# Attention into two feed-forward layers: one planner that also hands out six PSUM banks, new ranks, and another order of the first steps

## The chip, the cores and the metric

The kernel runs on one core of a Trainium2 chip. The metric is the device time of one execution in microseconds; the median of three runs of the kernel before is 1122.49 us (1120.99 to 1125.56). The core has five engines with a queue each: TensorE (PE, matrix products, with its weight loads shown as PEld), VectorE (DVE), ScalarE (ACT), GpSimd (POOL) and SyncE (SP, which here issues all DMAs). Matrix products land in PSUM, eight banks of 512 fp32 columns; the other data is in SBUF.

## The reference

Attention over batch 4, 8 heads, 576 positions, head size 64, with a decay that is added to the scores, and then two feed-forward layers over the 2304 tokens (512 to 2048 to 512, and 512 to 1536 to 512 with a gate). Cut to what matters:

```python
cum = np.cumsum(np.log(np.clip(f, 0.0001, 1.0)), axis=-1)
scores = scale * q @ k.T
scores = np.where(causal, -1e9, scores + cum[:, :, :, None] - cum[:, :, None, :])
scores = scores - scores.max(-1)
attn = np.exp(scores); attn = attn / (attn.sum(-1) + 1e-9)
x = attn @ v                              # then tokens x 512
h = x @ w_in;  x = (h * sigmoid(1.702 * h)) @ w_out
x = (silu(x @ w_gate) * (x @ w_val)) @ w_out2
```

The weights come in 64-bit floats, which the kernel turns into two fp32r parts (a high one and the rest) by itself.

## The kernel before

**Attention, by pairs of heads.** A pair P (0 to 15) holds two heads of one batch, in the two halves of the partitions; e is the head in the pair. `maxima(P)` records the work that finds the row maxima. Keys and queries come by DMA (`raw`), ACT casts them to a high part (`hi`, L264) and POOL subtracts for the rest (`lo`, L265). TensorE multiplies queries and keys and adds the decays `dk` (L272, L275) in four chunks of columns; all four use the one tile `mx` of two banks (one for each head). For each chunk DVE takes masked maxima out of the banks (L279, L295) into the tile `mt`. Then TensorE transposes `mt` with an identity ("turn", L308), once more into `mx`, and ACT copies the result to `selm` (L311). Since there is one `mx`, each chunk waits until DVE has read the one before, the turn waits for the last maxima, and the next pair's first chunk waits for ACT's copy.

`products(P)` records what uses the maxima: scores in four chunks with the decays and maxima as a fourth product (L326), into four banks `sc` used in turn; `exp` on ACT (L331); causal masks on POOL (L335); products with the values into `xx` (L356), row sums by a product with ones into the free columns of `xx` (L385); copies out of `xx` (L368, L389); and the division: sums to `rs` by DMA, a reciprocal on DVE (L400, L401), to DRAM and back spread over partitions (`rw`, `rb`), a product and a split into `xhi` and `xlo` (L408 to L411).

**The order.** Both functions only record operations with an engine, a duration, a rank, what they read and write, and a latency (`Program.add`). `Program.order` is a list scheduler: it keeps a clock for each engine and gives it, among the operations that are ready, the one with the lowest rank. The rank is P for products and P - 1.25 for maxima. The order that comes out is each engine's instruction order. The first steps (the logarithm of `f`, its running sum, its two parts `ahl`, and the DMAs that spread them to `dk`, as well as the table `selc` made by four transposes, L207 and L210) are recorded the same way.

**Weights.** Five weight tiles (of the 13 that fit) are loaded and converted during attention with a rank behind all else (`early`): a DMA of 512 KB, an absolute value on ACT (L461), four DVE operations (L463 to L468), a cast on ACT (L481) and a subtraction on POOL (L482). They may start at 100 us plus 12 us each by the scheduler's clock.

**The two feed-forward layers** (`moe`, L512 to L564) start when the sums of pair 15 are through TensorE. All tokens pass four chunks of four column tiles, later four of three, three fp32r products each; their weights are loaded and converted on the way. Nothing of this part is edited but the step size of a weight's conversion in `load_w`.

Of the kernel before, what the change touches and what calls it, by code (L numbers as in the profile page):

```python
# [17 lines left out]
NH = B * H  # L18
# [8 lines left out]
LOOK = 1.25  # L27
QH = 378
WHEN, WSTEP = 100000, 12000
# [9 lines left out]
class Program:  # L39
# [3 lines left out]
    def __init__(self):  # L43
        self.ops = []
        self.writer = {}
        self.readers = {}

    def add(self, eng, dur, rank, emit, reads=(), writes=(), lat=None, after=0):
        n = len(self.ops)
        deps = set()  # L50
        for k in reads:
            if k in self.writer:
                deps.add(self.writer[k])
# [12 lines left out]
        self.ops.append((eng, dur, rank, emit, sorted(deps), lat, after))  # L66

    def order(self):
# [40 lines left out]
def kernel(  # L109
# [18 lines left out]
    def f32(ap):  # L128
        return ap.bitcast(F32)
# [14 lines left out]
    prog = Program()  # L144
# [6 lines left out]
    NK, NR, NP, NV, NX, NB = 2, 2, 3, 2, 3, 2  # L151
# [6 lines left out]
    m5 = tiles(2, [128, 2], F32, "m5")  # L158
# [6 lines left out]
    rs = tiles(2, [128, 9], F32, "rs")  # L165
    rr = tiles(2, [128, 9], F32, "rr")
# [3 lines left out]
    da = pd.tile([NH, 2, S], F32, name="da")  # L170
# [7 lines left out]
    half = (slice(0, 64), slice(64, 128))  # L178

# [3 lines left out]
    def sp(rank, o, i, reads, writes, lat):  # L183
        add("sp", DMA_ISSUE, rank, lambda: nc.sync.dma_start(out=o, in_=i), reads, writes, lat=lat)
# [5 lines left out]
    sp(-9, ft, f, (), ["ft", ("xs", 0)], 2200)  # L190
    add("pool", 200, -9, lambda: nc.gpsimd.memset(zero, 0.0), (), ["zero", ("p", 2, 0)])
    add("pool", 300, -9, lambda: nc.gpsimd.affine_select(
        out=mk, in_=zero, pattern=[[-1, 128]], compare_op=ALU.is_ge, fill=NEG, base=0, channel_multiplier=1),
        ["zero"], ["mk", ("p", 2, 0)])
    add("pool", 500, -9, lambda: nc.gpsimd.affine_select(
        out=ident, in_=zero, pattern=[[-1, 128]], compare_op=ALU.not_equal, fill=1.0, base=0, channel_multiplier=1),
        ["zero"], ["ident", ("p", 2, 0)])
    add("dve", 1400, -9, lambda: nc.vector.memset(f32(mt), 0.0), (), ["mt0"])
    for q in range(4):
        for c in (4 * q, 66 + 4 * q):  # L200
            add("dve", 80, -9, lambda q=q, c=c: nc.vector.memset(f32(mt[:, q, :, c:c + 2]), 1.0), ["mt0"], [("mt1", q, c)])
    MT1 = [("mt1", q, c) for q in range(4) for c in (4 * q, 66 + 4 * q)]
    add("dve", 220, -9, lambda: nc.vector.tensor_copy(out=identr, in_=ident), ["ident", ("p", 2, 0)], ["identr"])

    def selectors():
        for q in range(4):
            nc.tensor.matmul(mx[:, q * 128:(q + 1) * 128], mt[:, q, 0, :], identr, start=True, stop=True)  # L207

    add("pe", 600, -9, selectors, ["identr"] + MT1, [("mx", 0)])
    add("act", 600, -9, lambda: nc.scalar.copy(out=selc.rearrange("p a b -> p (a b)"), in_=mx[:, 0:512]), [("mx", 0)], ["selc"])  # L210
    add("dve", 450, -9, lambda: nc.vector.memset(xx[:, 0:384], 0.0), (), ["xs0"])
    add("dve", 220, -9, lambda: nc.vector.memset(maskw[:, 0:384], 0.0), (), ["maskw0"])
    add("dve", 220, -9, lambda: nc.vector.tensor_copy(out=maskw[:, 384:512], in_=mk), ["mk", ("p", 2, 0)], ["maskw"])
    add("dve", 540, -10, lambda: nc.vector.memset(one, 1.0), (), ["one", ("xs", 1)])
    add("dve", 540, -10, lambda: nc.vector.tensor_scalar(
        out=ft, in0=ft, scalar1=1e-4, scalar2=1.0, op0=ALU.max, op1=ALU.min), (), ["ft", ("xs", 0)])
    add("act", 2000, -10, lambda: nc.scalar.activation(out=lf, in_=ft, func=AF.Ln), ["ft"], ["lf", ("xs", 2)])
    add("dve", 1350, -10, lambda: nc.vector.tensor_tensor_scan(
        out=cum, data0=one, data1=lf, initial=0.0, op0=ALU.mult, op1=ALU.add),
        ["one", "lf", ("xs", 1), ("xs", 2)], ["cum", ("rb", 0, 0)])  # L220
    add("dve", 520, -10, lambda: nc.vector.tensor_scalar(
        out=ft, in0=cum, scalar1=-8.0, scalar2=None, op0=ALU.mult), ["cum", ("rb", 0, 0)], ["ft", ("xs", 0)])
    add("dve", 800, -10, lambda: nc.vector.tensor_copy(out=ahl[0], in_=ft), ["ft", ("xs", 0)], ["ahl0", ("selm", 0)])
    add("dve", 750, -10, lambda: nc.vector.tensor_tensor(
# [442 lines left out]
```

## Time and profile before

| | |
|---|---|
| median of three runs | 1122.49 us |
| the profiled execution, its own time | 1123.12 us |
| its span, first to last instruction | 1121.1 us |
| attention (0 to the first product of the layers) | 265.8 us |
| the two layers | 855.3 us |
| TensorE busy | 1048.3 us, 94% |
| DVE, ACT, POOL busy | 623.2, 360.8, 182.4 us |

The profiled execution has 2.0 us outside its span and lies 0.6 us above the median. The layers keep TensorE at work nearly without a gap, the attention stage does not. For matrix products the view's durations overlap their neighbours, as they are pipelined; the distance between two starts is what one costs.

### The profile page before, as it was taken

How to read it: one execution, taken by the hardware profiler on the slowest of the kernel's cores; microseconds unless marked ns; L12 is line 12 of the kernel's file. 1: busy time of each engine (PE TensorE's matmuls, PEld its weight loads, DVE VectorE, ACT ScalarE, POOL GpSimd, SP SyncE). 2: the span in 40 equal slices, each digit the busy share in tenths (PEclk: the TensorE clock that was granted, in tenths of full speed). 3: DMA queues.
4: the chain of work that ended last, by engine and by line, in shares of the span. 5: the costliest groups of instructions: out<-in, count | busy, mean ns of one | idle time of the engine just before them, and what ended most of it. 6: DMA issues, size and time to landing. Idle time of an engine off the chain costs nothing.

```text
span 1121.1 us, 15630 instructions
## 1 busy us (share of the span) xinstructions
PE 1048.3 (94%) x6212; PEld 860.2 (77%) x6212; DVE 623.2 (56%) x1227; ACT 360.8 (32%) x648; POOL 182.4 (16%) x262
## 2 busy tenths in 40 slices
PE   2888777889999999999999999999999999999998
PEld 1666656667688788878877888888888888888886
DVE  5456756552966835664485578337733863363333
ACT  1455444443524313332343343123212321221110
POOL 4333343331201100200020011002100210010000
PEclk9999888999999999999999999999999999999999
DMA  3133353210221300220021012002200220000101
GB/s 121 45 103 114 97 165 105 96 47 23 79 72 38 113 1 1 75 75 1 19 95 37 1 57 95 1 1 77 93 1 1 88 82 1 1 0 29 48 19 75
DMA packets 25464, 61.43 MB, mean 55 GB/s; under 512 B 7760, under 2 KB 8272, under 8 KB 25392
## 3 DMA queue, kind: packets, MB, share of 16 engines
q1 hardware_dynamic: 25392, 60.45, 17.0%
q8 instruction: 48, 0.79, 0.3%
q14 instruction: 24, 0.20, 0.1%
HBM read 55.35 MB, written 4.94 MB: 54 GB/s over the span
## 4 chain that ended last, share of the span: by engine, by line
PE 80%; DVE 12%; ACT 2%; issue 2%; DMA 2%; POOL 1%; SPq 1%; ACTq 0%; DVEq 0%; POOLq 0%
PE ps L513 22%; PE ps L514 22%; PE ps L512 22%; PE sc L326 5%; PE xx L356 4%; PE mx L272 2%; DVE cvt L466 2%; DVE junk L279 2%; PE xx L385 2%; DVE cvt L468 2%; PE mx L275 1%; DVE cvt L464 1%; DVE cvt L463 1%; DVE g L526 1%; DVE s L534 1%
## 5 line engine op out<-in xcount | busy, mean ns | idle before, releaser
L512 PE MATMUL ps<-xhi,w 128*128 128x512 f32 (+1 forms) x800 | 294.5, 368 | 0.0
L513 PE MATMUL ps<-xlo,w 128*128 128x512 f32 (+1 forms) x800 | 294.4, 368 | 0.0
L514 PE MATMUL ps<-xhi,w 128*128 128x512 f32 (+1 forms) x800 | 294.2, 368 | 0.0
L513 PE MATMUL ps<-g,w 128*128 128x512 f32 (+1 forms) x560 | 207.5, 371 | 3.1 <-DVE g L526 3.1
L512 PE MATMUL ps<-g,w 128*128 128x512 f32 (+1 forms) x560 | 206.1, 370 | 3.7 <-ACT g L525 3.6
L514 PE MATMUL ps<-g,w 128*128 128x512 f32 (+1 forms) x560 | 206.1, 368 | 0.5 <-POOL w L482 0.5
L482 POOL TENSOR_TENSOR w<-cvt,w 128x512 fp32r<-128x512 f32 x68 | 89.4, 1319 | 664.8 <-ACT w L481 648.4
L532 ACT ACTIVATE t<-ps 128x512 f32<-128x512 f32 (+1 forms) x140 | 77.5, 554 | 298.4 <-PE ps L514 297.5
L512 PEld LDWEIGHTS ps<-xhi,w 128*128 128x128 f32 x800 | 150.8, 189 | 25.2
L514 PEld LDWEIGHTS ps<-xhi,w 128*128 128x128 f32 x800 | 150.8, 188 | 25.1
L513 PEld LDWEIGHTS ps<-xlo,w 128*128 128x128 f32 x800 | 150.8, 189 | 24.9
L534 DVE SCALAR_TENSOR_TENSOR s<-t,ps 128x512 f32<-128x512 f32 (+1 forms) x140 | 88.4, 631 | 123.9 <-ACT t L532 123.0
L525 ACT CAST g<-s 128x512 fp32r<-128x512 f32 (+1 forms) x140 | 81.0, 578 | 182.9 <-DVE s L546 129.4
L513 PEld LDWEIGHTS ps<-g,w 128*128 128x128 f32 x560 | 105.6, 189 | 24.5 <-DVE g L526 7.4
L512 PEld LDWEIGHTS ps<-g,w 128*128 128x128 f32 x560 | 105.4, 189 | 24.6 <-ACT g L525 7.3
L559 DVE SCALAR_TENSOR_TENSOR acc<-ps,acc 128x512 f32<-128x512 f32 (+1 forms) x120 | 76.0, 636 | 84.9 <-PE ps L514 84.2
L526 DVE TENSOR_TENSOR g<-s,g 128x512 fp32r<-128x512 f32 (+1 forms) x140 | 92.0, 658 | 54.1 <-ACT g L525 53.4
L514 PEld LDWEIGHTS ps<-g,w 128*128 128x128 f32 x560 | 105.6, 189 | 17.9 <-POOL w L482 0.9
L279 DVE CUSTOM_DVE_ANT_0 junk<-mx,maskw 128x512 bf16<-128x512 f32 (+3 forms) x128 | 61.8, 483 | 38.2 <-PE mx L275 36.2
L331 ACT ACTIVATE p<-sc 128x512 f32<-128x512 f32 (+2 forms) x128 | 56.4, 504 | 34.9 <-PE sc L326 34.6
L335 POOL TENSOR_SCALAR_AFFINE_SELECT p<-p 128x128 f32<-128x128 f32 (+1 forms) x160 | 43.9, 290 | 144.7 <-ACT p L331 143.6
L546 DVE TENSOR_TENSOR s<-s,ps 128x512 f32<-128x512 f32 (+1 forms) x60 | 38.0, 633 | 46.0 <-PE ps L514 45.7
(70 smaller groups left out, 1029.5 us busy)
## 6 DMA issues: line engine op xcount, KB each, us to landing
raw<-in_kq_dram SPq DMA_DIRECT2D x16, 576.0 KB
stg<-in_w_dram SPq DMA_DIRECT2D x16, 512.0 KB
stg<-in_w1o_dram SPq DMA_DIRECT2D x16, 512.0 KB
stg<-in_wg_dram SPq DMA_DIRECT2D x12, 512.0 KB
stg<-in_wv_dram SPq DMA_DIRECT2D x12, 512.0 KB
stg<-in_w2o_dram SPq DMA_DIRECT2D x12, 512.0 KB
vr<-in_v_dram SPq DMA_DIRECT2D x16, 320.0 KB
rb<-rw SPq DMA_DIRECT2D x32, 144.0 KB
```

What stands on the lines that cost most here:

```text
L279: nc.vector.tensor_tensor_reduce(out=junk[:, 0:n], in0=mx[:, e * 512 + o:e * 512 + o + n], in1=maskw[:, end - n:end], scale=1.0, scalar=fl ...
L326: nc.tensor.matmul(bank[e][:, o:o + n], w[half[e]], x[half[e]], start=w.tensor is h_.tensor and x.tensor is h_.tensor, stop=x.tensor is sm ...
L331: nc.scalar.activation(out=ps[e][:, a:z], in_=sc[c % 2][e][:, 0:z - a], func=AF.Exp, scale=0.125)
L482: nc.gpsimd.tensor_tensor(out=w[:, 1, :], in0=st, in1=f32(w[:, 0, :]), op=ALU.subtract)
L512: nc.tensor.matmul(o, wh, rh, start=i == 0, stop=False)
L513: nc.tensor.matmul(o, wh, rl, start=False, stop=False)
L514: nc.tensor.matmul(o, wl, rh, start=False, stop=i == n - 1)
L525: nc.scalar.copy(out=g[:, 0, 0:n], in_=s)
L526: nc.vector.tensor_tensor(out=g[:, 1, 0:n], in0=s, in1=f32(g[:, 0, 0:n]), op=ALU.subtract)
L532: nc.scalar.activation(out=t, in_=o, func=AF.Tanh, scale=scale)
L534: nc.vector.scalar_tensor_tensor(out=s, in0=t, scalar=1.0, in1=o, op0=ALU.add, op1=ALU.mult)
L559: nc.vector.scalar_tensor_tensor(out=a, in0=o, scalar=0.5, in1=a, op0=ALU.mult, op1=ALU.add)
```

## The change

The change has four parts. (1) The tiles `mx` and `sc` go; six banks are given out by the scheduler itself: an operation can take banks and give them back, at most four for maxima or for scores (`CAP`), and it is not ready until enough are free. (2) The ranks come from a table with a number for each kind of operation; the four value products rank 1.12 behind their own pair's scores. The turn is split in two (blocks 0 to 3, and block 4), with a copy each; there are four tiles `p` in place of three, so both heads of two pairs have their own. (3) The first steps: `ahl` comes straight from the running sum without a copy between, `mt` is set block by block, the four DMAs of the first `dk` follow one another ahead of `da`, an exponential of one column on ACT follows the logarithm, keys and values of the first pairs are recorded with a start time, and so are the `lo` subtractions. (4) The early weights may start at 143.7 us plus 8.4 us each by the scheduler's clock, and each of their DVE operations is scheduled by itself.

```diff
-LOOK = 1.25
+RANK = dict(raw=-3.17, v=-1.93, hi=-3.28, lo=-0.4, max=-0.89, maxv=-1.25, turn=-2.59, sm=-1.25, score=0, exp=0,
+            mask=-0.12, pv=1.12, ev=1.74, sum=1.14, ss=1.17, div=0.39, mul=1.13, xhi=1, xlo=2.07)
+CAP = 4
-WHEN, WSTEP = 100000, 12000
+WHEN, WSTEP = 143700, 8400
...
+        def at(n):
+            k = len(ops[n][7])
+            if not k:
+                return ready_at[n]
+            if len(spare) < k or held.get(ops[n][7][0][0], 0) + k > CAP:
+                return 1e12
+            return max(ready_at[n], spare[k - 1][0])
...
-                now = max(free.get(eng, 0), min(ready_at[n] for n in pool))
+                now = max(free.get(eng, 0), min(at(n) for n in pool))
...
+            for k in o[7]:
+                self.bank[k] = spare.pop(0)[1]
+                held[k[0]] = held.get(k[0], 0) + 1
+            for k in o[8]:
+                spare.append((now + o[1] + o[5], self.bank[k]))
+                held[k[0]] -= 1
...
-    NK, NR, NP, NV, NX, NB = 2, 2, 3, 2, 3, 2
+    NK, NR, NP, NV, NX, NB = 2, 2, 4, 2, 3, 2
...
-    mx = pm.tile([128, 1024], F32, name="mx")
-    sc = [[pm.tile([128, 512], F32, name=f"sc{i}{e}") for e in range(2)] for i in range(2)]
+    bank = [pm.tile([128, 512], F32, name=f"bank{i}") for i in range(6)]
...
+    add("act", 1400, -19, lambda: nc.scalar.activation(out=m5[:, 0, 0:1], in_=m5[:, 0, 0:1], func=AF.Exp), ["lf", "m50"])
...
-        out=ft, in0=cum, scalar1=-8.0, scalar2=None, op0=ALU.mult), ["cum", ("rb", 0, 0)], ["ft", ("xs", 0)])
-    add("dve", 800, -10, lambda: nc.vector.tensor_copy(out=ahl[0], in_=ft), ["ft", ("xs", 0)], ["ahl0", ("selm", 0)])
-    add("dve", 750, -10, lambda: nc.vector.tensor_tensor(
-        out=ahl[1], in0=ft, in1=f32(ahl[0]), op=ALU.subtract), ["ft", ("xs", 0), "ahl0"], ["ahl1", ("selm", 1)])
+        out=ahl[0], in0=cum, scalar1=-8.0, scalar2=None, op0=ALU.mult), ["cum", ("rb", 0, 0)], ["ahl0", ("selm", 0, 0)])
+    add("dve", 750, -20, lambda: nc.vector.scalar_tensor_tensor(
+        out=ahl[1], in0=cum, scalar=-8.0, in1=f32(ahl[0]), op0=ALU.mult, op1=ALU.subtract),
+        ["cum", ("rb", 0, 0), "ahl0"], ["ahl1", ("selm", 1, 0)])
...
+    add("pe", 1000, -14, selectors, ["identr", ("mt1", 0)], take=[("sel",)])
+    add("act", 600, -14, lambda: nc.scalar.copy(out=selc.rearrange("p a b -> p (a b)"), in_=bk("sel")), (), ["selc"],
+        give=[("sel",)])
...
+        def first(c, dur, *parts):
+            add("pe", dur, P + RANK["max"], lambda: rmm(c, *parts), KM, take=[("mx", P, c, e) for e in range(2)])
...
-        add("pe", 400, RM, turn, [("mt", hp, t, e) for t in range(5) for e in range(2)] + ["identr"] + MT1, MB)
-        add("act", 660, RM, lambda: nc.scalar.copy(out=sm, in_=mx[:, 0:S]), MB, [("selm", im)])
+        for c, ts in enumerate(((0, 1, 2, 3), (4,))):
+            n = 512 - 448 * c
+            add("pe", 110 * len(ts), P + RANK["turn"], lambda c=c, ts=ts: turn(c, *ts),
+                [("mt", hp, t, e) for t in ts for e in range(2)] + ["identr"], take=[("turn", P, c)])
+            add("act", 170 + n * .8, P + RANK["sm"], lambda c=c, n=n: nc.scalar.copy(
+                out=sm[:, 512 * c:512 * c + n], in_=bk("turn", P, c)[:, 0:n]), (), [("selm", im, c)], give=[("turn", P, c)])
...
-        add("pe", c4(448, 128), R0, lambda: pv((0, 512, 128, 448, True, False), (0, 384, 0, 128, True, True)), kp(0, 1), ["xx"])
+        add("pe", c4(448, 128), P + RANK["pv"], lambda: pv((0, 512, 128, 448, True, False), (0, 384, 0, 128, True, True)), kp(0, 1), ["xx"])
```

**ACT at the start of the program.** `selc` is the table of four transposes, `xs2 <- xs0` is the logarithm, `hi` the high part of keys and queries. Before:

```order
L217 ACT_TABLE_LOAD
L217 ACTIVATE xs2_94<-xs0_92 32x576
L210 CAST selc_83<-mx_112 128x512
L264 CAST hi0_74<-raw0_72 128x2x576
L264 CAST hi1_75<-raw1_73 128x2x576
L311 CAST selm0_84<-mx_112 128x576
L331 ACT_TABLE_LOAD
```

After:

```order
L253 ACT_TABLE_LOAD
L253 CAST selc_82<-bank0_109 128x512
L229 ACT_TABLE_LOAD
L229 ACTIVATE xs2_94<-xs0_92 32x576
L230 ACT_TABLE_LOAD
L230 ACTIVATE m5_81<-m5_81 128x1
L293 CAST hi0_74<-raw0_72 128x2x576
L293 CAST hi1_75<-raw1_73 128x2x576
```

The copy of `selc` has moved ahead of the logarithm, with a table load of its own, and the casts of `hi` stand behind a third table load.

**TensorE around the turn of a pair** (`identr,mt` is the turn, `hi` and `dk,selc` a chunk of the maxima, `xx` with `ones` the row sums, `sc` scores). Before, from the last chunk of pair 1's maxima on:

```order
L272 MATMUL mx_112<-hi1_75 128x320 x2
L275 MATMUL mx_112<-dk0_78,selc_83 128x320 x2
L308 MATMUL mx_112<-identr_109,mt_80 128x128 x4
L308 MATMUL mx_112<-identr_109,mt_80 128x64
L272 MATMUL mx_112<-hi0_74 128x512 x2
L275 MATMUL mx_112<-dk0_78,selc_83 128x512 x2
L326 MATMUL sc00_113<-hi1_75 128x512
L326 MATMUL sc01_114<-hi1_75 128x512
```

After, from the end of the row sums of pair 3 on:

```order
L425 MATMUL xx_115<-p2_90,ones32_105 32x64
L425 MATMUL xx_115<-p3_91,ones32_105 32x64
L343 MATMUL bank1_110<-identr_106,mt_80 128x128 x4
L343 MATMUL bank3_112<-identr_106,mt_80 128x64
L301 MATMUL bank5_114<-hi0_74 128x512
L301 MATMUL bank0_109<-hi0_74 128x512
L304 MATMUL bank5_114<-dk1_79,selc_82 128x512
L304 MATMUL bank0_109<-dk1_79,selc_82 128x512
L301 MATMUL bank4_113<-hi0_74 128x128
L301 MATMUL bank2_111<-hi0_74 128x128
L304 MATMUL bank4_113<-dk1_79,selc_82 128x128
L304 MATMUL bank2_111<-dk1_79,selc_82 128x128
```

The last chunk of the maxima has moved from directly ahead of the turn to ahead of the row sums. Behind the turn come two chunks of maxima in four other banks, and behind them the value products of the pair before and only then the scores.

**DVE where attention ends** (`rs` and `rr`, or `rsr`, the reciprocal of pair 15's sums; `cvt` a weight's conversion; `s` the first result of the layers). Before:

```order
L400 TENSOR_SCALAR rs1_98<-rs1_98 128x9
L401 RECIPROCAL rr1_100<-rs1_98 128x9
L408 TENSOR_TENSOR rb1_102<-xs0_92,rb1_102 128x576
L411 TENSOR_TENSOR xlo_59<-rb1_102,xhi_58 128x576
L534 SCALAR_TENSOR_TENSOR s_2748<-t_2746,ps_2733 128x512
L534 SCALAR_TENSOR_TENSOR s_2777<-t_2775,ps_2762 128x512
```

After, from the same reciprocal on:

```order
L439 TENSOR_SCALAR rsr_97<-rsr_97 128x9
L440 RECIPROCAL rsr_97<-rsr_97 128x9
L502 TENSOR_SCALAR cvt_2711<-cvt_2711 128x512
L505 TENSOR_SCALAR cvt_2711<-cvt_2711 128x512
L509 SCALAR_TENSOR_TENSOR cvt_2711<-stg_2694,cvt_2711 128x512
L513 SCALAR_TENSOR_TENSOR cvt_2711<-stg_2694,cvt_2711 128x512
L502 TENSOR_SCALAR cvt_2722<-cvt_2722 128x512
L505 TENSOR_SCALAR cvt_2722<-cvt_2722 128x512
```

The conversions of the fourth early weight (w1 tile 3) and of the fifth have moved behind the reciprocal of pair 15, which waits for a DMA; before, all five stand further ahead, among the maxima.

## Rows read from the trace of the kernel before

**Rows 1.** Busy time by stretch: start:end, length, engines (instructions), clock, DMA
```profile
31.50:256.61 225.11, 186.71 (x1995) 139.59 (x1995) 129.25 (x413) 107.16 (x204) 84.92 (x169) 0.93 0.31 96
...
72.97:86.58 13.61, 11.63 (x133) 8.70 (x133) 7.27 (x26) 6.76 (x14) 5.35 (x11) 1.00 0.29 96
...
230.15:243.78 13.63, 11.65 (x134) 8.71 (x135) 7.27 (x26) 6.76 (x14) 5.33 (x11) 1.00 0.17 48
...
130.89:173.46 42.57, 31.81 (x268) 23.98 (x268) 25.48 (x69) 17.69 (x34) 14.80 (x25) 0.70 0.45 132
...
256.61:265.77 9.16, 9.03 (x105) 6.41 (x104) 1.51 (x4) 4.70 (x10) 2.68 (x10) 1.00 0.14 33
...
265.77:1121.10 855.33, 844.29 (x4084) 708.95 (x4080) 477.09 (x770) 243.58 (x428) 83.07 (x63) 1.00 0.13 42
```

**Rows 2.** Instructions in time, one pair: start, length, engine, work, [idle]
```profile
73.52 0.76 DVE L411 TENSOR_TENSOR xlo<-rb,xhi 128x576 fp32r<-128x576 f32 x1 [1.41 <-ACT xhi L410]
...
73.54 0.39 PE L326 MATMUL sc<-hi 64*128 64x512 f32 x2
...
73.77 0.39 PE L326 MATMUL sc<-lo,hi 64*128 64x512 f32 x2
...
81.72 1.65 PE L385 MATMUL xx<-p,ones 128*32 128x378 f32 x32
...
83.90 0.55 DVE L279 CUSTOM_DVE_ANT_0 junk<-mx,maskw,m 128x320 bf16<-128x320 f32 x1 [1.76 <-PE mx L275]
...
85.11 0.74 PE L308 MATMUL mx<-identr,mt 128*128 128x128 f32 x5 [1.25 <-DVE mt L279]
...
85.89 0.64 ACT L311 CAST selm<-mx 128x576 fp32r<-128x576 f32 x1 [1.44 <-PE mx L308]
...
86.58 0.50 PE L272 MATMUL mx<-hi 64*128 64x512 f32 x2 [0.73 <-ACT selm L311]
```

**Rows 3.** The same view, the start of the program
```profile
2.00 2.19 DVE L198 MEMSET mt<- 128x2560 f32 x1 [0.48 <-issue]
...
5.34 0.69 ACT L217 ACTIVATE xs<-xs 32x576 f32<-32x576 f32 x1 [3.26 <-DVE xs L215]
...
6.06 1.34 DVE L218 TENSOR_TENSOR_SCAN rb<-xs,xs 32x576 f32<-32x576 f32 x1
...
6.22 0.59 ACT L210 CAST selc<-mx 128x512 fp32r<-128x512 f32 x1 [0.19 <-PE mx L207]
...
7.94 5.99 POOL L265 TENSOR_TENSOR lo<-raw,hi 128x1152 fp32r<-128x1152 f32 x2 [1.22 <-ACT hi L264]
...
8.40 3.06 DVE L224 TENSOR_TENSOR selm<-xs,selm 32x576 fp32r<-32x576 f32 x1
...
16.00 0.65 SPq L184 DMA_DIRECT2D dk<-selm  x1
...
18.92 0.76 PE L275 MATMUL mx<-dk,selc 64*128 64x512 f32 x1 [2.64 <-DMA dk<-selm]
...
19.72 0.69 DVE L279 CUSTOM_DVE_ANT_0 junk<-mx,maskw 128x512 bf16<-128x512 f32 x1 [8.26 <-PE mx L275]
...
31.46 1.28 ACT L331 ACT_TABLE_LOAD   x1
...
32.52 0.63 PE L326 MATMUL sc<-hi 64*128 64x512 f32 x2
...
32.94 0.63 PE L326 MATMUL sc<-lo,hi 64*128 64x512 f32 x2
```

**Rows 4.** TensorE by stretch: length, busy (instructions), clock, DMA share, GB/s
```profile
126.00:128.00 2.00, 0.56 (x4) 1.00 0.96 248
...
130.00:132.00 2.00, 1.27 (x8) 0.50 0.13 42
```

**Rows 5.** Instructions in time, start of the two expert layers
```profile
271.42 0.17 DVE L400 TENSOR_SCALAR rs<-rs 128x9 f32<-128x9 f32 x1 [3.15 <-DMA rs<-ss]
...
289.12 0.50 PE L514 MATMUL ps<-g,w 128*128 128x512 f32 x1 [0.47 <-POOL w L482]
```

More of the change, by code (lines that the diff above doesn't have):

```diff
@@ L46, in __init__, with add @@
         self.readers = {}
-    def add(self, eng, dur, rank, emit, reads=(), writes=(), lat=None, after=0):
+        self.banks = banks
+        self.bank = {}
+    def add(self, eng, dur, rank, emit, reads=(), writes=(), lat=None, after=0, take=(), give=()):
         n = len(self.ops)
         deps = set()
+        reads, writes = list(reads) + list(give), list(writes) + list(take)
         for k in reads:
@@ L80, in order @@
         free = {}
+        spare = [(0, i) for i in range(self.banks)]
+        held = {}
         out = []
+        def at(n):
[5 more added lines that the diff above has]
+            return max(ready_at[n], spare[k - 1][0])
         while any(pools.values()):
@@ L157 @@
     mt = ap_.tile([128, 4, 5, 128], F32R, name="mt")
-    m5 = tiles(2, [128, 2], F32, "m5")
+    m5 = ap_.tile([128, 2, 2], F32, name="m5")
     selc = ap_.tile([128, 4, 128], F32R, name="selc")
@@ L199 @@
[L199 to L203, printed above, removed]
+    add("pool", 100, -20, lambda: nc.gpsimd.memset(m5, 0.0), (), ["m50", ("m5", 0, 0), ("m5", 0, 1)])
+    add("dve", 540, -20, lambda: nc.vector.memset(one, 1.0), (), ["one", ("xs", 1)])
@@ L205, in selectors @@
+    add("dve", 220, -14, lambda: nc.vector.tensor_copy(out=identr, in_=ident), ["ident", ("p", 2, 0)], ["identr"])
     def selectors():
         for q in range(4):
[L207 to L211, printed above, removed]
@@ L270, in rmm @@
+        add("act", 1160, P + RANK["hi"], lambda: nc.scalar.copy(out=h_[:, :, 0:S], in_=r), [("raw", ir)], [("hi", ik)])
+        add("pool", 2900, P + RANK["lo"], lambda: nc.gpsimd.tensor_tensor(
+            out=l_[:, :, 0:S], in0=r, in1=f32(h_[:, :, 0:S]), op=ALU.subtract), [("raw", ir), ("hi", ik)], [("lo", ik)], after=11000)
+        def rmm(c, *parts):
             for o, i, k0, n in parts:
                 for e in range(2):
-                    nc.tensor.matmul(mx[:, e * 512 + o:e * 512 + o + n], h_[half[e], 1, i * 128:(i + 1) * 128],
+                    nc.tensor.matmul(bk("mx", P, c, e)[:, o:o + n], h_[half[e], 1, i * 128:(i + 1) * 128],
@@ L317, in products, with smm @@
         ps = [pt[(2 * P + e) % NP] for e in range(2)]
         ip = [(2 * P + e) % NP for e in range(2)]
-        def smm(bank, parts):
-            for o, j, q0, n in parts:
+        def smm(c):
+            bank = [bk("sc", P, c, e) for e in range(2)]
+            for o, j, q0, n in parts[c]:
                 ks = slice(j * 128, (j + 1) * 128)
```

207 lines of the change are left out of this document (111 added, 96 removed).

## The prediction

> **What bounds the kernel now.** I read the page's busy times first, then busy time by stretch, then one pair and the start of the program in order of time. The page puts TensorE at 94% of the span (the table above). By stretch this splits: in the two feed-forward layers, 855.3 us, TensorE is busy for 844.3; the attention stage is where it idles [rows 1]. Attention has three parts: 32.5 us until the first score product starts [rows 3], with little TensorE work; fifteen periods, from 31.50 to 256.61, that take 225.1 us; and the last pair, 9.16 us with 9.03 busy, up to the layers at 265.77 [rows 1].
>
> A regular period lasts 13.61 to 13.63 us with 11.63 to 11.65 of TensorE work, DVE 7.27, ACT 6.76, POOL 5.35 [rows 1]. So TensorE bounds it, and what is left over is two waits: 1.25 us ahead of the turn for the last maxima of DVE, and 0.73 ahead of the next pair's maxima for ACT's copy of the turn [rows 2]. 11.63 + 1.25 + 0.73 = 13.61: nothing else is open in a regular period.
>
> The fifteen periods hold 186.7 us of TensorE busy time and 225.1 - 186.7 = 38.4 idle [rows 1]. At full clock the work would be 15 x 11.63 = 174.5, so 12.2 us are lost to half clock. Of the idle time 15 x 1.98 = 29.7 are the two regular waits, and 8.7 are longer ones, most of them where early weights are converted: from 130.89 to 173.46 two periods take 42.6 us, at a mean granted clock of 0.70 [rows 1]. The clock falls to its lower level, 1.2 GHz, in 130 to 132, after a stretch in which TensorE was busy for 0.56 of 2 us [rows 4].
>
> **The change, part by part.**
>
> *The start.* The chain to the first decays loses one of the two short DVE operations between 7.40 and 8.40, and its last one is freed from POOL: it took 3.06 us beside `lo` [rows 3], while one of the same width without company takes 0.76 [rows 2]. But the order on ACT puts the copy of `selc` ahead of the logarithm. It started at 6.22 behind a filling of all five blocks of `mt`, 2.19 us [rows 3]; one block makes it 1.75 earlier, so its end comes at 5.05. Then a table load, 1.28 like the one in the trace [rows 3], and the logarithm runs from 6.35 to 7.05 where it ran from 5.34 to 6.03. Running sum 1.34, first part 0.5, second part 0.76: done at 9.65, before at 11.46. (`lo` can't disturb it: behind the logarithm stand another table load and a cast of 1.1, together 2.4 us, against 1.84 until the second part starts.) The four DMAs go out one behind the other, 0.65 us of issue each, the last at 10.85; before, it went out at 16.00, behind loads of keys that waited for `lo`, and its product started 2.9 us later [rows 3]. So 13.75 in place of 18.92, and DVE starts on the maxima at 14.0 or so in place of 19.72.
>
> From there DVE sets the pace, since four chunks find free banks at once. Of its 7.27 us in a period 2 x 0.76 go to the division's last two steps and some 0.4 to the reciprocal, so maxima are 5.4, with small gaps 5.9: pair 0 is through at 19.9. Its turn and copies (0.74 and 0.64, [rows 2]) go beside the first maxima of pair 1, and the first scores need a bank that two of these (1.4 us with gaps) still hold, and a little more: 21.8. Before it was 32.52 [rows 3]. The gain is 10.7 us, and three of four chunks of pair 1's maxima are then done, where before it was one. Bounds: 19 if the logarithm is not held back, 28 if the chain were hardly shorter.
>
> Here a page speaks against the change. The Trainium skill, "ScalarE: Activation LUTs", section "What ACT_TABLE_LOAD costs", gives a switch of tables 1.28 us for the load and 1.38 more for draining; the load agrees with the trace's 1.28, the drain can't be seen there, as the activation behind each load waited for something else. By the page the first scores would come 1.4 us later.
>
> *The wait ahead of the turn* goes. The last chunk of maxima now stands ahead of the row sums: DVE needs 1.15 us for it (two of 0.55 and what lies between), the sums take 1.6 [rows 2], and the first half of the turn does not even need that chunk. If that cover goes (a DVE operation in front that waits for a DMA), what DVE is late beyond 0.4 us comes back as the same wait.
>
> *The wait ahead of the next maxima* goes as well: they have other banks. What waits for ACT's copy now is the scores; ahead of them stand two chunks of maxima and the first value products, over 2 us of TensorE work, so the copy (0.64, a little more as it is two) is hidden with 1 us to spare. That the value products follow a pair late costs nothing by itself: it is the same work, and with four `p` tiles exp has room to write.
>
> *New waits by banks.* A score chunk takes the banks of the first maxima of the same period, some 2.3 us after TensorE filled them; DVE needs 1.4 for each. A maxima chunk takes those of scores whose exp has had over 1 us. Each has about 1 us of slack. DVE at 7.3 and ACT at 6.9 us are at 63% and 59% of 11.63, so they don't bound, but they work in order: a reciprocal that waits for its DMA holds back the maxima behind it. I bound the new waits over the fifteen periods by 0 and by 30 (half of the 29.7, the 8.7 and half of the 12.2); the nearest rows are the regular periods, which show no wait outside the two known, so I take 0.4 us a period, 6.
>
> *The early weights* start some three pairs later and sit in the last three. Four of the five conversions stand behind the last maxima on DVE and so can't hold TensorE up inside attention. The price comes at the start of the layers: the fourth tile is converted behind pair 15's reciprocal, which waited for its DMA until 271.42, 5.65 us after attention's end [rows 5]. With an estimated 4 us more on DVE, ACT and POOL it is ready 9.7 us after that end, and it is wanted after 36 products at the 0.23 of [rows 2], 8.3 us. Four tiles of the second kind are wanted from 14 us on; the last came 23.3 us after the end before [rows 5], and some 2 later now, as its DMA goes out behind pair 15's. I take 2.5 us, within 0 and 5.
>
> *The sum.* End of attention: 21.8 (first scores) + 174.5 (fifteen pairs' work) + 9.0 (last pair) - 2.0 (three chunks of pair 1's maxima are done by then, some 0.65 each, by 0.57 for the first: from 72.97, one period ahead of 86.58, to the scores at 73.54, [rows 2]) + 1.2 (first scores at the low clock: 0.42 for a 512-column step, [rows 3], where 0.23 is usual, [rows 2]) + 6 (new waits) = 210.5; before 265.8. The layers: 855.3 + 2.5 = 857.8. Span 1068.3, and with the 2.0 us outside it 1070.3 against 1123.1 of the profiled execution, which lies 0.6 above the median. I say 1070.
>
> **The rivals.**
>
> *The waits come back in another dress.* The scheduler hands out banks by estimated durations, while engines and DMAs keep their own; queues in order turn one late DMA into a late bank. For it: the 8.7 us of irregular waits that the scheduler before left. Against it: the regular periods, equal to 0.02 us [rows 1]. Then the new waits are 20 to 30: 1084 to 1098, say 1090.
>
> *The first decays come hardly earlier.* `selc` ahead of the logarithm and three table loads in place of two eat the gain; scores at 28, the rest as forecast: 1076. For it: the order on ACT. Against it: the last DMA of `dk` no longer stands behind loads that need POOL.
>
> *The clock, which would make it slower.* In the new order TensorE changes between short groups, each with its bank to wait for. If small gaps between them kept it at 1.2 GHz, a step would take 0.42 in place of 0.23, 1.8 times as long; a pair run so costs 0.8 x 11.63 = 9.3 us more. The 53 us of gain, and 0.5% beyond, are used up from six to seven pairs of the sixteen on; with half of the pairs the time is 1145. For it: two periods of the trace that ran at 0.70 of the clock [rows 1]. Against it: the regular periods have gaps of 0.73 and 1.25 each and stay at 1.00 [rows 1, 2], and the fall came after TensorE was mostly idle [rows 4]. The Trainium skill has such a rule in "TensorE: Matmul & The Clock Gate", section "A second HAM failure mode: psum-queue depth-cycling": a kernel that goes round the PSUM banks can idle in small pieces between groups and swing between the two levels. The regular periods, which go round six banks as well, don't agree.
>
> **How the numbers follow.** Forecast 0.65 (own range 1058 to 1084); waits that come back 0.20; no earlier start 0.09; clock 0.04; the remaining 0.02 is a gain lost in a way that I don't see. The lower end is the sum with the first scores at 19, no new waits and no loss in the layers: 1070 - 2.8 - 6 - 2.5, rounded down to 1058. The upper end has new waits of 30 and 5 us in the layers: 1070 + 24 + 2.5, rounded up to 1098. Half a per cent, 5.6 us, is about what a measurement of this kernel tells from no change. Faster by more than that 0.94, within it 0.02, slower 0.04.
>
> **What would show it.** Right: periods of 11.7 to 12.2 us in the middle of attention with TensorE over 95% busy, no wait of the turn for DVE over 0.5 us, first scores at 19 to 24, the first product of the layers at 205 to 218, clock 1.00 from 30 us on, and a wait for the fourth weight tile soon after the layers begin. Wrong: periods over 13 us, with DVE or ACT named as what ended TensorE's waits; a stretch at half clock in mid attention; first scores after 26; layers that take over 862 us.

## The result, and the profile after

The changed kernel takes 1078.07 us (median of 4 runs, 1077.65 to 1078.47) against 1121.74 (1120.47 to 1125.56) in the same series: ratio 0.9604, 95% interval 0.9578 to 0.9629. The forecast was 1070. The profiled execution takes 1078.47, its span is 1076.8. By stages, with what was forecast:

| | before | forecast | after |
|---|---|---|---|
| first scores | 32.52 | 21.8 | 22.32 |
| first product of the layers | 265.8 | 210.5 | 209.1 |
| layers | 855.3 | 857.8 | 867.7 |
| span | 1121.1 | 1068.3 | 1076.8 |

The attention came out within 1.4 us of the forecast; the layers lost 12.4 us where 2.5 were forecast. Busy time by stretch of the changed kernel, columns as in [rows 1]: one period of the attention, the attention from the first scores on, the layers, and the layers' first 61 us.

```profile
122.81:134.48 11.67, 11.67 (x137) 8.28 (x134) 7.45 (x26) 7.04 (x14) 5.66 (x12) 1.00 0.35 103
...
22.32:209.10 186.78, 185.04 (x2082) 131.62 (x2080) 114.34 (x391) 108.94 (x220) 88.30 (x176) 1.00 0.32 95
209.10:1076.80 867.70, 849.48 (x4082) 712.79 (x4080) 490.98 (x792) 248.46 (x436) 87.67 (x66) 0.99 0.15 46
209.10:270.00 60.90, 50.50 (x196) 38.87 (x195) 53.74 (x85) 26.46 (x46) 15.27 (x11) 0.89 0.44 138
```

A period is now as long as TensorE's work in it, 11.67 us, at clock 1.00. In 186.78 us of attention TensorE idles for 1.74. In the layers it idles for 867.70 - 849.48 = 18.2 us, before for 11.0 [rows 1], and its busy time grew by 5.2 for the same products: part of the first 61 us ran at a lower granted clock (0.89 on the mean). So of the 12.4 us some 7.2 are waits and some 5.2 are work at the lower clock.

One pair in time, the rows that answer to [rows 2]:

```profile
121.23 1.65 PE L425 MATMUL xx<-p,ones 128*32 128x378 f32 x32
...
122.03 0.55 DVE L308 CUSTOM_DVE_ANT_0 junk<-bank,maskw,m 128x320 bf16<-128x320 f32 x1
...
122.81 0.74 PE L343 MATMUL bank<-identr,mt 128*128 128x128 f32 x5
...
123.48 0.50 PE L301 MATMUL bank<-hi 64*128 64x512 f32 x2
123.51 0.70 ACT L349 CAST selm<-bank 128x512 fp32r<-128x512 f32 x2
```

The turn stands flush behind the sums, as the last maxima ended under them, and the next maxima flush behind the turn, while ACT copies the turn. Both regular waits are gone. The start, against [rows 3]:

```profile
4.72 0.59 ACT L253 CAST selc<-bank 128x512 fp32r<-128x512 f32 x1 [2.64 <-PE bank L250]
5.32 1.28 ACT L229 ACT_TABLE_LOAD   x1
6.62 0.68 ACT L229 ACTIVATE xs<-xs 32x576 f32<-32x576 f32 x1
...
9.19 0.75 DVE L236 SCALAR_TENSOR_TENSOR selm<-rb,selm 32x576 fp32r<-32x576 f32 x1
...
12.90 1.44 PE L304 MATMUL bank<-dk,selc 64*128 64x512 f32 x2 [2.21 <-DMA dk<-selm]
...
22.32 0.63 PE L366 MATMUL bank<-hi 64*128 64x512 f32 x2
22.75 0.63 PE L366 MATMUL bank<-lo,hi 64*128 64x512 f32 x2
```

`selc` does hold back the logarithm (6.62, forecast 6.35), the second decay part takes 0.75 beside nothing, and the decays' product starts at 12.90 (forecast 13.75).

The loss sits at the layers' start. TensorE's longest waits there:

```profile
219.56 0.50 PE L559 MATMUL ps<-xhi,w 128*128 128x512 f32 x1 [2.04 <-ACT w L526]
...
221.11 0.77 PE L561 MATMUL ps<-xhi,w 128*128 128x512 f32 x1 [0.57 <-POOL w L529]
...
232.82 0.80 PE L559 MATMUL ps<-g,w 128*128 128x512 f32 x1 [5.06 <-ACT g L572]
```

The first two are the fourth weight tile. The third, 5.06 us, is a wait for the first `g`, the gated output that the layers' second products read. What VectorE did meanwhile, and ScalarE's step that the gated output needs (L579):

```profile
215.75 0.17 DVE L439 TENSOR_SCALAR rsr<-rsr 128x9 f32<-128x9 f32 x1 [1.32 <-DMA rsr<-ss]
...
216.94 0.69 DVE L509 SCALAR_TENSOR_TENSOR cvt<-stg,cvt 128x512 uint32<-128x512 uint32 x1
...
219.96 1.65 DVE L509 SCALAR_TENSOR_TENSOR cvt<-stg,cvt 128x512 uint32<-128x512 uint32 x1
...
226.08 0.74 DVE L447 TENSOR_TENSOR rb<-xs,rb 128x576 f32<-128x576 f32 x1
...
228.00 0.58 ACT L579 ACTIVATE t<-ps 128x512 f32<-128x512 f32 x1
...
228.24 0.42 DVE L502 TENSOR_SCALAR cvt<-cvt 128x512 f32<-128x512 f32 x1
...
231.44 1.27 DVE L581 SCALAR_TENSOR_TENSOR s<-t,ps 128x512 f32<-128x512 f32 x2
```

The first product of the gated output (L581, 231.44) stands behind the division of pairs 14 and 15 (L447 and what follows it) and a weight conversion (L502 to L513). Its input from ScalarE was there at 228.58, so the conversion alone, which began behind the division, held it for 2.9 us. Pair 15's product ran at 226.08, 17.0 us after the attention's end; before, the same step came 11.3 us after it, with nothing of the weights in front, and the gated output's product right behind its division:

```profile
277.10 0.76 DVE L408 TENSOR_TENSOR rb<-xs,rb 128x576 f32<-128x576 f32 x1 [5.25 <-DMA rb<-rw]
...
278.60 0.76 DVE L411 TENSOR_TENSOR xlo<-rb,xhi 128x576 fp32r<-128x576 f32 x1 [0.74 <-ACT xhi L410]
...
279.27 1.51 DVE L534 SCALAR_TENSOR_TENSOR s<-t,ps 128x512 f32<-128x512 f32 x2
...
280.66 1.19 PE L512 MATMUL ps<-g,w 128*128 128x512 f32 x4 [0.99 <-ACT g L525]
```

VectorE has hardly a gap from 220 to 235 (4.90, 4.83 and 4.88 of 5 us). TensorE's clock fell to the lower level, 1.2 GHz, three times, each time behind such waits: for the tile (0.66 on the mean of 220 to 225, where a step takes 0.43 us), for the first `g` (0.64 and, up to 240, 0.68), and once more behind two later waits for `g`, 0.91 and 0.51 us at 258.96 and 261.10 (0.83 in 260 to 270):

```profile
220.00:225.00 5.00, 4.43 (x13) 3.20 (x12) 4.90 (x6) 1.31 (x2) 2.34 (x2) 0.66 0.94 248
...
230.00:235.00 5.00, 1.67 (x3) 1.06 (x4) 4.88 (x7) 3.44 (x7) 2.25 (x2) 0.64 0.29 105
...
260.00:270.00 10.00, 9.09 (x31) 6.83 (x32) 8.23 (x15) 2.50 (x5) 1.29 (x1) 0.83 0.39 117
```

### The profile page after: what moved, and what is told of

The parts are those of the page before. It is cut to its first block, busy times and chain, and to the rows that moved or that the text cites. A ratio compares the mean times of both kernels' runs of the same rounds, so it can differ in the third digit from the quotient of the medians.

```text
span 1076.8 us, 15837 instructions
## 1 busy us (share of the span) xinstructions
PE 1045.6 (97%) x6212; PEld 852.7 (79%) x6212; DVE 620.7 (58%) x1262; ACT 365.6 (34%) x666; POOL 184.0 (17%) x259
## 4 chain that ended last, share of the span: by engine, by line
PE 85%; DVE 9%; ACT 2%; issue 1%; POOL 1%; SPq 1%; DMA 1%; POOLq 0%; DVEq 0%; ACTq 0%
PE ps L560 23%; PE ps L561 23%; PE ps L559 22%; PE bank L366 6%; PE xx L396 4%; PE xx L425 2%; DVE cvt L509 2%; PE bank L301 2%; DVE cvt L513 1%; PE bank L304 1%; DVE cvt L505 1%; DVE g L573 1%; PE bank L343 1%; DVE cvt L502 1%; DVE s L581 1%
## 5 line engine op out<-in xcount | busy, mean ns | idle before, releaser
L529 POOL TENSOR_TENSOR w<-cvt,w 128x512 fp32r<-128x512 f32 x68 | 90.2, 1331 | 660.0 <-ACT w L526 638.7
L579 ACT ACTIVATE t<-ps 128x512 f32<-128x512 f32 (+1 forms) x140 | 77.5, 554 | 303.4 <-PE ps L561 302.6
L581 DVE SCALAR_TENSOR_TENSOR s<-t,ps 128x512 f32<-128x512 f32 (+1 forms) x140 | 88.3, 632 | 124.7 <-ACT t L579 123.9
L308 DVE CUSTOM_DVE_ANT_0 junk<-bank,maskw 128x512 bf16<-128x512 f32 (+3 forms) x128 | 62.5, 488 | 31.3 <-PE bank L304 22.5
L371 ACT ACTIVATE p<-bank 128x512 f32<-128x512 f32 (+2 forms) x128 | 58.5, 502 | 46.6 <-PE bank L366 43.0
L500 ACT ACTIVATE cvt<-stg 128x512 f32<-128x512 f32 x68 | 46.1, 677 | 48.3 <-POOL w L529 44.3
```

The source lines that it names most:

```text
L308: nc.vector.tensor_tensor_reduce(out=junk[:, 0:n], in0=bk("mx", P, c, e)[:, o:o + n], in1=maskw[:, end - n:end], scale=1.0, scalar=floor, ...
L371: nc.scalar.activation(out=ps[e][:, a:z], in_=bk("sc", P, c, e)[:, 0:z - a], func=AF.Exp, scale=0.125)
L529: nc.gpsimd.tensor_tensor(out=w[:, 1, :], in0=st, in1=f32(w[:, 0, :]), op=ALU.subtract)
L579: nc.scalar.activation(out=t, in_=o, func=AF.Tanh, scale=scale)
L581: nc.vector.scalar_tensor_tensor(out=s, in0=t, scalar=1.0, in1=o, op0=ALU.add, op1=ALU.mult)
```

## The experiments

**What carries the attention's gain.** Three runs undo the two halves of the new planning, the free banks and the ranks a pair behind. `two_banks`:

```diff
-CAP = 4
+CAPS = dict(mx=2, sc=4)   # maxima, turns, selectors together: 2
```

> The changed kernel with the six banks split as before: maxima, their turns and the selectors together hold at most two, scores at most four; the ranks stay. Theory: the periods fell from 14.6 to 11.67 us because maxima no longer wait for their two banks; with two banks the regular waits of TensorE on VectorE's maxima come back, a period is 13 to 14.6 us, the first scores come 1 to 3 us later, and the time is 1100 to 1130. Rival: the value products ranked a pair behind fill these waits, so a period stays under 12.2 us and the time under 1090.

`pv_now`:

```diff
-pv=1.12, ev=1.74, sum=1.14, ss=1.17
+pv=0, ev=0, sum=0, ss=0
```

> The changed kernel with value products, sums and their copies ranked with their own pair (pv, ev, sum and ss = 0), the banks free as in the change. Theory (the banks carry the gain, the ranks fill what is left): TensorE waits for the exponentials and masks of its own pair, 0.3 to 1 us a period; the period is 11.9 to 12.7 us, the time 1082 to 1095. Rival (the ranks behind carry the gain): period 13.5 us or more, time 1105 or more.

`two_banks_pv` has both edits.

> Both undone: maxima, turns and selectors on two banks, and value products, sums and their copies ranked with their own pair. The first alone cost 27.6 us (1105.7), the second alone 34.7 (1112.8). Theory: banks and ranks hide the same waits, each needs the other, so the two losses do not add: the period is that of before, 14 to 15 us, the time 1110 to 1125. Rival: they are separate waits and add up, time 1130 to 1145.

Measured: 1105.72 us (ratio to before 0.9827, interval 0.9784 to 0.9871), 1112.82 (0.9892, 0.9849 to 0.9935) and 1104.91 (0.984, 0.98 to 0.988). Attention from the first scores on and layers, one fence for each kernel (the profiled executions took 1107.77, 1106.71 and 1103.30 us; of `pv_now` the other three took 1111.26 to 1116.16, so its stages are those of its fastest):

```profile
21.10:242.98 221.88, 200.68 (x2097) 142.55 (x2096) 128.88 (x413) 111.84 (x229) 90.64 (x179) 0.95 0.32 96
242.98:1106.10 863.12, 846.92 (x4083) 711.78 (x4080) 479.48 (x774) 243.47 (x428) 83.22 (x63) 0.99 0.14 43
```
```profile
22.30:243.35 221.05, 203.65 (x2083) 142.00 (x2079) 139.51 (x412) 110.87 (x228) 94.81 (x179) 0.95 0.33 96
243.35:1105.00 861.65, 846.88 (x4084) 711.32 (x4080) 476.24 (x771) 243.28 (x428) 83.72 (x63) 0.99 0.14 43
```
```profile
21.10:246.53 225.43, 202.07 (x2097) 144.03 (x2096) 132.14 (x416) 110.24 (x229) 91.01 (x179) 0.94 0.34 98
246.53:1101.60 855.07, 844.34 (x4083) 708.94 (x4080) 477.32 (x770) 243.61 (x428) 83.32 (x63) 1.00 0.13 42
```

Against the 186.8 us of the change the three stages take 35.1, 34.3 and 38.7 more; before it was 265.8 - 32.5 = 233.3, 46.5 more. So of the 46.5 us either half alone keeps some 12, and neither keeps 8. For `two_banks` the theory held but for the first scores, which came 1.2 us sooner and not later; for `pv_now` the rival; the losses of the two don't add, as the third expectation has it, though its time lies below the range. Banks and ranks are one measure. The other ranks were left as they were chosen for the free banks, so part of these losses can be an order that doesn't fit; no run separates that. Where the waits are in the attention of the first and second of them (who waits for whom: total us, times, longest):

```profile
PE bank L350 <- DVE mt L315: 18.6, 12, 4.8
```
```profile
PE bank L343 <- DVE mt L308: 6.3, 7, 2.0
PE bank L301 <- DVE mt L308: 6.2, 7, 2.1
```

In both it is DVE's maxima that come late (L350 and L343 are the turn). (L301 is a chunk of the maxima.) These waits are 18.6 of 35 us and 12.5 of 34; 15.6 and 18.6 us are longer busy time for the same work, at a clock of 0.95 on the mean (1.00 in the change). The third run also bears on the layers: with the change's own weight times they take 855.1 us there, as before. An attention that ends 37 us later has the conversions done, and pair 14's broadcasts go out ahead of pair 15's sums (243.91 and 247.68 on SyncE), whose product comes 11.0 us after the attention's end. The late end alone doesn't do it: in `pv_now`, where the conversions are done as well, pair 14's broadcasts go out amid pair 15's sums, the product comes 14.2 us after the end, and the layers take 861.7.

**First theory of the layers' loss: late weights.** `w_early` has the weight times of before, `w_mid` something between:

```diff
-WHEN, WSTEP = 143700, 8400
+WHEN, WSTEP = 100000, 12000    # w_mid: 125000, 8400
```

> The changed kernel, with the two numbers that time the early weights set back to those of before (WHEN, WSTEP = 100000, 12000). Theory: of the 12.4 us that the layers lost (867.7 against 855.3), nearly all comes from weight conversions that are still on VectorE and ScalarE when the attention ends; with all five tiles converted by then the layers take 854 to 859 us, the attention still ends at 208 to 212 us, and the time is 1064 to 1071. Rival one: the layers are late because pair 15's own divisions and the w1o tiles meet at the attention's end, whatever the five tiles do: layers stay above 863 and the time above 1073. Rival two: the conversions, now amid the attention, cost what they save: attention's end at 214 or later.

> The changed kernel with WHEN, WSTEP = 125000, 8400: the early weights start some 19 us sooner in the planner's time than in the change, and 25 us later than in the first run. Theory: the layers' loss follows how many conversions are left at the attention's end, so it lies between the two: layers 855 to 864 us, time 1065 to 1074. Rival (the loss comes from pair 15's divisions and the w1o tiles): layers as in the changed kernel, 866 to 869 us, time 1076 to 1079.

Measured: 1074.49 us (0.9557, 0.9535 to 0.9579) and 1077.58 (0.9584, 0.9564 to 0.9605). The first interval touches the change's (0.9578 to 0.9629), the second overlaps it; the stages tell more. With `w_early` the attention ends at 212.19, 3.1 later (1.2 of them a wait of the turn for maxima behind conversions; the rest isn't traced to a row), and the layers take 860.6: better by 7.1, not by 12. With `w_mid` they take 867.6, TensorE waits 9.1 us for the first `g`, and pair 15's product 3.73 for its broadcast's DMA, while two weight tiles load (the DMA engines are busy for 0.97 and 0.93 of 224 to 228). Neither forecast of `w_early` held; of `w_mid` the rival's numbers did. So late weights are a good half of the loss, the attention takes part of it back, and 5.3 us over the 855.3 of before are something else; moving the weights only a little gains nothing. In `w_early`, with no conversion left there, the first gated output still stands behind pair 15's division, 12.6 us after the end, as pair 14's two broadcasts now go out among pair 15's sums. Over the kernels TensorE's wait for the first `g` grows with the lateness of pair 15's product behind the attention's end: 0.64 us for a product at 11.0 (`two_banks_pv`), 0.99 at 11.3 (before), 2.2 at 12.6 (`w_early`), 3.9 at 14.2 (`pv_now`), 5.1 at 17.0 (the change), 7.1 at 17.4 (`two_banks`), 9.1 at 19.5 (`w_mid`). The rows of `w_early`:

```profile
224.75 0.76 DVE L447 TENSOR_TENSOR rb<-xs,rb 128x576 f32<-128x576 f32 x1 [4.61 <-DMA rb<-rw]
...
226.92 1.51 DVE L581 SCALAR_TENSOR_TENSOR s<-t,ps 128x512 f32<-128x512 f32 x2
```

**Second theory: the queues' order.** The division's sums go through memory and back (four DMAs of sums, reciprocal, one DMA, two broadcasts) while its engines' queues stand. `div_pool` moves the last steps of two pairs to GpSimd; `w_early_div` does so with earlier weights:

```diff
-add("dve", 850, P + RANK["mul"], ...)       # and xhi on ACT, xlo on DVE
+if P >= 14: three steps as nc.gpsimd.tensor_tensor, add("pool", 1350, ...)
```

> The changed kernel with its late weights, but the three steps of the division of pairs 14 and 15 (product, high part, low part) on GpSimd instead of VectorE and ScalarE. Theory, formed after the first runs: what the layers lose is mostly the queue's order. The first gated outputs (tanh on ScalarE, product on VectorE) stand behind pair 15's division, which waits for its broadcast sums from memory, and that round trip takes longer since the change; so with the division elsewhere TensorE's wait of 5.06 us for the first g falls under 2, the late fourth weight tile (2.0 and 0.6 us) stays, layers 859 to 865 us, time 1069 to 1075. Rival (the four conversions themselves keep VectorE busy): the wait stays over 4 us, time 1076 to 1080.

> The same division on GpSimd, and the early weights at WHEN, WSTEP = 60000, 12000, so that all five are converted some three pairs before the attention ends. Theory: no conversion and no division is left in front of the first gated outputs; the waits of TensorE for g at the layers' start go under 1.5 us together, the clock stays at 1.00, the layers take 851 to 857 us, the attention ends at 208 to 211, the time is 1061 to 1068. Rival (w1o tiles and the bare work of the layers' start are the limit): layers 859 us or more, time 1070 or more.

Measured: 1082.84 us (0.9638, 0.9604 to 0.9672) and 1075.70 (0.9589, 0.9544 to 0.9633). Both theories missed, and the time of `div_pool` lies above its rival's range too: TensorE's longest wait for `g` grew to 8.19 us in `div_pool` and is 4.12 in `w_early_div`, whose attention ends only at 215.56. The rows of GpSimd, ScalarE and TensorE in `div_pool` say why:

```profile
231.16 1.40 POOL L452 TENSOR_TENSOR xlo<-rb,xhi 128x576 fp32r<-128x576 f32 x1
232.51 1.26 POOL L537 TENSOR_TENSOR w<-cvt,w 128x512 fp32r<-128x512 f32 x1
...
233.81 0.66 ACT L508 ACTIVATE cvt<-stg 128x512 f32<-128x512 f32 x1 [10.14 <-POOL w L537]
...
235.55 1.65 PE L567 MATMUL ps<-g,w 128*128 128x512 f32 x3 [8.19 <-ACT g L580]
```

GpSimd's low part of a weight tile (L537) now stands behind the division, ScalarE's next conversion (L508) waits 10.14 us for the buffer that this frees, and the high part of `g` (L580) stands behind it. The head of the line had only changed engines: VectorE's gated output came at 226.91 in place of 231.44, but ScalarE couldn't pass it on. So the theory's place was right and its remedy wrong: VectorE, ScalarE and GpSimd all feed the layers.

**The wait covered instead.** `deeper` leaves all queues and gives TensorE other work:

```diff
+if lay == 1 and c == 0 and bi == 1 and i == c:
+    for j in (i + 1, i + 2):
+        ahead[j] = first(wt["w1", j], t0, n)   # before the first products with g
```

> The changed kernel with two first products of the layers' second block (24 matmuls, 5.4 us at full clock) put on TensorE ahead of the first second products, which wait for g; the division, the weights and the queues of the other engines stay. Theory: the wait of 5.06 us for the first g is a wait for pair 15's division at the head of two queues, at a fixed time, so other work in front of it covers it: the wait falls under 0.8 us, the clock doesn't fall a second time, layers 860 to 863 us, time 1071 to 1074. Rival (VectorE's backlog of conversions sets the pace of the layers' first 60 us): TensorE waits later for the next g or weight instead, layers 865 us or more, time 1076 or more.

Measured: 1069.05 us (0.9526, 0.9489 to 0.9564), an interval that lies below the change's 0.9578 to 0.9629. The layers take 858.4 us. TensorE's waits in the layers:

```profile
PE ps L560 <- DVE g L573: 3.3, 8, 0.5
...
PE ps L559 <- ACT w L526: 1.9, 1, 1.9
PE ps L559 <- ACT g L572: 1.8, 4, 0.5
```

The longest wait for `g` is 0.5 us where it was 5.1, and the clock falls once (220 to 225, 0.66), not three times. What remains is mostly the tile's wait, 1.9 and 0.6, with the fall behind it. The gain, 9.3 us of 867.7, is more than the wait and the forecast: TensorE idles for 5.9 us less, and its busy time is 3.5 shorter (846.0 for 849.5), as the second and third fall went too. So 9.3 of the 12.4 us are gone once TensorE has other work while the queues stand behind pair 15's division and the conversion that follows it.

**The start.** `ln_first` makes the copy of `selc` wait for the logarithm; `warm` adds 26 matmuls that nothing reads while TensorE waits for the decays:

```diff
+["lf"] in the reads of selc's copy
+18 x nc.tensor.matmul(bk("warm")[:, 0:128], identr, identr)  # behind the selectors
+ 8 x the same, between pair 0's first maxima product and the decays' product
```

> The changed kernel with one more dependency: the copy of the selectors waits for the logarithm. In the changed kernel the copy stands first on ScalarE, at 4.72 us, and the table load for the logarithm comes behind it, at 5.32. Theory: the table is then loaded at 0.8 us while nothing else could run, the logarithm starts at 4.1 to 4.3 instead of 6.62, and all behind it moves by 2 to 2.5 us: first scores at 19.8 to 20.8 instead of 22.32, time 1075 to 1077. Rival: pair 0's high part, now behind the exponential's table and the copy, or its low part on GpSimd, is next: first scores at 21.5 or later, time 1077 to 1079.

> The kernel with the logarithm ahead of the selectors, and 26 matmuls of 128 columns whose results nothing reads: 18 behind the selector product, 8 between pair 0's first maxima product and the decays' product, so that TensorE is busy from 3.6 us on where it was idle for 6 us. Theory: without them the first scores came 3 us sooner (19.3), but their steps took 0.43 us in place of 0.23 up to 31 us, where those of the changed kernel did so up to 26.4, and the lead was gone; with TensorE busy from the start the steps take 0.23 from 20 us on or sooner, pair 1's first scores come at 27 to 30 us (33.1 without, 32.4 in the changed kernel), the attention ends at 203 to 207, the time is 1070 to 1074. Rival: the clock stays low until some 31 us whatever TensorE does before, or the maxima on VectorE are the pace of the first pairs: the attention ends at 208 or later, time 1075 or more.

Measured: 1076.60 us (0.9581, 0.9541 to 0.9621) and 1075.54 (0.9585, 0.9547 to 0.9623); by the times alone no difference from the change. In its profile the first scores of `ln_first` came at 19.30, 3.0 sooner, but pair 1's at 33.12, and the attention ended at 209.84, 0.7 later. Its steps of 384 columns and the first of pair 1's scores, and busy times with the clock:

```profile
17.11 0.49 PE L301 MATMUL bank<-hi 64*128 64x384 f32 x2
17.34 0.59 PE L304 MATMUL bank<-dk,selc 64*128 64x384 f32 x2
...
33.12 0.41 PE L366 MATMUL bank<-hi 64*128 64x512 f32 x2
```
```profile
14.00:16.00 2.00, 1.47 (x7) 0.63 (x5) 1.97 (x9) 0.00 (x0) 0.00 (x0) 1.00 0.88 269
16.00:18.00 2.00, 1.76 (x12) 1.26 (x12) 1.57 (x7) 0.59 (x1) 0.00 (x0) 0.87 0.99 337
18.00:20.00 2.00, 2.00 (x13) 1.94 (x15) 1.70 (x6) 0.21 (x1) 0.00 (x0) 0.50 0.45 182
```

TensorE was already at 2.4 GHz there: the step from 17.11 to 17.34 takes 0.23 us, where the same step takes 0.42 in the change (20.08 to 20.50). Then, after two waits for VectorE's maxima (0.42 and 0.35 us, TensorE busy for 1.47 and 1.76 of 2 us), the clock fell to 1.2 GHz before 18 and stayed there until 31, and the lead was gone. This is one execution, of 1079.84 us at a mean clock of 0.987; the other three took 1075.71 to 1076.84 at 0.991 to 0.994, so they need not have had this fall, and what the order alone gives stays open.

In `warm` pair 1's scores come at 30.08:

```profile
30.08 0.40 PE L375 MATMUL bank<-hi 64*128 64x512 f32 x2
```

The attention ends at 206.81 there, 2.3 sooner than in the change. Steps still take 0.43 us up to 23.5 (26.4 in the change). With this start pair 1's scores come at 29.86 to 30.24 in three profiles (`warm` and the two kernels below), with the change's start at 31.19 to 32.42 in six (the change, `w_early`, `w_mid`, `div_pool`, `w_early_div`, `deeper`). How much of that is the order and how much the matmuls isn't shown.

**Together.** `best` joins `deeper`, `warm` and weights at 90000, 12000; `deeper_warm` keeps the change's weight times.

> All together: logarithm first, the 26 matmuls, the two first products ahead, and the early weights at WHEN, WSTEP = 90000, 12000. Theory: attention's end at 205 to 209 (early weights cost it 2 to 3 us), layers 855 to 859, time 1062 to 1069, less than both kernels. Rival: each gain is taken back by the next wait, time 1070 or more.

> The two first products ahead, the logarithm first and the 26 matmuls, with the weights timed as in the change. Theory: the two gains lie in different stages and add up: attention's end at 206 to 207.5 us as with the 26 matmuls alone, layers 857 to 860 us as with the products ahead alone, time 1065 to 1069. Rival: an earlier attention's end only lengthens the wait for the late fourth weight tile, time 1069 to 1071.

Measured: 1072.28 us (0.9555, 0.9517 to 0.9592) and 1065.84 (0.9492, 0.9465 to 0.9518). `best` missed its theory: it has the shortest layers of all, 853.4 us, and pays for it with an attention that ends at 216.93; its longest wait there is 3.0 us, for ScalarE's copy of a turn (L358, at 178.07), which stands behind a conversion that waited for its weight tile's DMA:

```profile
177.50 0.66 ACT L509 ACTIVATE cvt<-stg 128x512 f32<-128x512 f32 x1 [4.30 <-DMA stg<-in_w1o_dram]
```

It is the same mechanism once more, inside the attention.

`deeper_warm` ends the attention at 206.6 and takes 857.5 us for the layers, as its parts did and as its theory has it; its interval lies below the change's and overlaps that of `deeper`, and it is the fastest kernel of the study.

## Why the prediction was right, and where it was not

- *The start*: right. 22.32 for 21.8, each step within 0.9 us. The Trainium skill, "ScalarE: Activation LUTs", section "What ACT_TABLE_LOAD costs", adds 1.38 us of draining to each switch of tables. This trace shows the load and no drain behind it: the load at 5.32 takes 1.28, ends at 6.60, and the logarithm starts at 6.62; the measurement decides.
- *First scores at the low clock*: 1.2 forecast. The steps took 0.43 until 26.4, four microseconds at half speed, so some 2. The attention's 1.4 us are a balance: its work from the first scores on took 185.0 us where the sum has 182.7, the start came 0.5 later, and the new waits were 4.3 shorter.
- *Both regular waits* gone: right, and for the reasons given (rows of the pair above); `two_banks` brought back 18.6 us of waits for maxima. But of the value products a pair late the prediction said only that it "costs nothing by itself: it is the same work". `pv_now` lost 34 us: with free banks that rank is what keeps TensorE at work while DVE finishes the maxima.
- *New waits*: 6 forecast, bounds 0 and 30. TensorE idled for 1.74 us, and two waits are named, 0.8 and 0.7 in the last 20 us. Banks planned by estimated durations held. (By its own terms the rival of the waits ends at 1094, or 1096.5 with 5 us in the layers, not at 1098.)
- *The clock's rival* didn't come: 1.00 through the whole attention from 40 us on, though TensorE goes round six banks in short groups. The swing that the Trainium skill describes in "TensorE: Matmul & The Clock Gate", section "A second HAM failure mode: psum-queue depth-cycling", comes with small idle pieces between the groups. Here TensorE idled for 1.74 of 186.78 us, and the swing isn't there.
- *The early weights in the attention*: that they hold up nothing there was right (`w_early` and `best` show what they cost when they do).
- *The layers' start* is the step that failed. "I take 2.5 us, within 0 and 5", for a fourth tile ready 9.7 us after the end. The tile's part was nearly right: its high part came 10.4 us after the end, and the waits are 2.04 and 0.57 where the sum had 1.4. What the sum lacked is the queue behind pair 15's division. In the trace of before the division's last step ran from 278.60 and the gated output's product from 279.27: hardly any slack, and TensorE waited 0.99 us for its first `g` even then. The prediction read the reciprocal in [rows 5] and asked only which tile was late behind it, not what else stood in those queues, nor that late weights would stand among the division's own steps. The product came 5.7 us later (17.0 for 11.3; 12.6 in `w_early`, so most of it is the weights and the rest pair 14's division, which now overlaps), a conversion got in front of the gated output, TensorE waited 5.06 and then ran at half clock. `deeper`, which only gives TensorE other work there, takes 9.3 of the 12.4 us back. 867.7 is above the 862 that was named as proof of error.

That the total still fell inside the range is luck as far as this step goes: the 9.9 us by which the layers missed their forecast used the room that the range kept for new waits in the attention, which didn't come.

## What to carry to other kernels

Where a stage ends in a round trip through memory, list everything that stands behind its last step in each engine's queue, and by how much that step was early before: a tie costs as soon as anything delays the trip. Here it was better to give the bounding engine other work across such a wait than to move the waiting step to another queue. A start that comes sooner can be lost to a fall of the clock right behind it: measure where pair 1 starts, not pair 0, and in more than one profile.

## What the runs showed of the hardware

- In the change the granted clock reads 1.00 from the start while its steps until 26.4 take 0.43 us; in `ln_first` it reads 1.00 before 14 us, with steps of 0.42, and at 17.11, with a step of 0.23. At the start of a program the steps tell the level, not that column.
- In one execution (`ln_first`) the clock, which had risen to 2.4 GHz (a step of 0.23 us at 17.11), fell back to 0.50 by 18 us, behind two waits of TensorE for maxima (0.42 and 0.35 us), and stayed there until 31.
- A VectorE conversion step of 128x512 takes 0.69 us (L509 at 216.94) and 1.65 when GpSimd subtracts at the same time (219.96; GpSimd's L529 runs from 219.59 for 1.47). Four weight tiles in a row so cost VectorE more than their single steps suggest.
